# Queries of the first three batches loaded four tokens to a row, in a retention and bilinear feed-forward kernel

## The chip, the cores and the metric

One Trainium2 chip, one core. The time is device microseconds of one execution; the median of three runs of the kernel before is 325.34 us (325.18 to 326.11). The core has TensorE (matrix products, one instruction after another in the order of its queue), VectorE, ScalarE and GpSimd (elementwise work), and SyncE, which here only issues transfers. ScalarE and GpSimd issue transfers too. Each engine works through its own queue in order; an instruction that waits holds up everything behind it on that engine.

## What is computed

Eight batches, eight heads, 576 tokens, 64 features to a head, all inputs float32:

```
scores = q @ k^T / 8
gamma[h] = 1 - 2^(-5 - h)
D[h, s, t] = gamma[h]^(s - t)  for s >= t, else 0
x = (scores * D) @ v                      # per batch and head
x -> rows of 512 (all heads of a token), 4608 rows
out = ((x @ w_a) * (x @ w_b)) @ w_out     # 512 -> 1536 -> 512
```

## The kernel before, in words

The kernel works in bf16 with float32 sums. The decay is split: v is scaled by gamma^(-t) (table `vs`), the product's result by gamma^s / 8 (table `qs_o` for the first 256 tokens of a batch, `qs` later), and between them only a mask of zeros and ones is left. Attention runs in blocks of tokens; what lies in earlier blocks comes in through a running state (k^T v, 64 x 64 per head). The feed-forward part takes the resulting `xT` in blocks of 512, 256, 256 and then 512 tokens: products `pa` with `w_a` and `pb` with `w_b`, ScalarE copies `pa` out (L868), VectorE multiplies (L880), and `po` is the product with `w_out` (L896), copied out to `osb` and stored by SyncE. Attention of later batches is slipped into these products by a list of due times (`todo`), counted in TensorE cost.

**The opening.** The first 256 tokens of batches 0, 1 and 2 go another way than the rest, in steps: `STEPS` lists (batch, half of the heads); steps 0 and 2 are batch 0, steps 1 and 3 are batch 1, steps 4 and 5 are batch 2. Steps 0 to 3 are written out by hand, in the order in which the lines from L929 on stand; steps 4 and 5 are in `todo` (`early_casts`, `third_turn`, `third_states`, `third_outputs`). A step loads q, k and v of its four heads with two tokens to a row of SBUF: partition p holds tokens 2p and 2p + 1, 512 bytes together, so a transfer of 256 KB has 512 pieces of 512 bytes (L159). The steps' transfers stand in a row in SyncE's queue, except the first k, which ScalarE issues:

```
for i, which in ((0, Q), (0, K), (0, V), (2, Q), (2, K), (1, K),
                 (1, Q), (2, V), (3, K), (3, Q), (1, V), (3, V)):
```

Then, for each step: `cast_step` turns q and k into bf16, even tokens before odd ones (L316); `values_step` scales v (L324 on ScalarE, L326 elsewhere); `transpose_step` turns q and k, 128 x 128 at a time, on TensorE into PSUM (L334), and copies them out (L338); `score_step` makes 16 products of keys and queries (L352) and multiplies by the mask on VectorE (L360, `sT`); `state_step` makes k^T v (L379), and ScalarE copies the state that a later block needs (L391) and keeps sums (L395, L396); `output_step`, or its parts `open_step`, `step_states` (L449), `step_keys` (L465) and `close_step` (L481, L486), makes the outputs and writes them scaled into `xT`. Even tokens stand before odd ones everywhere, in the mask, in `qs_o`, in `xT` and so in the rows of `osb`; `store` undoes it with two transfers of 64 rows, every second row of the output (L791).

`last_states` makes the state products of steps 1 and 3 together and copies them out (L412 to L416). After the outputs of steps 1 and 3 the first feed-forward products begin: `ffn_begin` for the first 256 tokens (batch 0), `begin_with` for the next 256 (batch 1), both L811, with the first piece of `w_a`; the first `pb` (L875) follows.

`warm` puts products of ones into TensorE's queue (L923), whose results nobody reads. The weights are loaded in pieces through GpSimd's queue (`load_w`, `load_wo`), cast to bf16 on the way, in an order that stands between GpSimd's casts and value products.

PSUM: `ps_ffn` has four buffers of one bank for everything tagged `ab`; `ps_sc` and `ps_o` have one buffer of two banks each (the scores of a step, and the outputs of a step or the first two `pa`).

Of the kernel before, what the change touches and what calls it, by code (L numbers as in the profile page):

```python
# [10 lines left out]
FP32 = mybir.dt.float32  # L11
# [7 lines left out]
def kernel(  # L19
# [134 lines left out]
    def load_step(n, hh, which, on=nc.sync):  # L154

        if n not in paired:
            paired[n] = [stage.tile([128, 2 * DM], FP32, tag=name, name=name)
                         for name in ("qf", "kf", "vf")]
        on.dma_start(  # L159
            paired[n][which][:, hh * DM:(hh + 1) * DM]  # L160
            .rearrange("p (h e) -> p h e", h=4),
            (q, k, v)[which][n, 4 * hh:4 * hh + 4, 0:256, :]
            .rearrange("h (p two) d -> p h (two d)", two=2))
# [3 lines left out]
    for i, which in ((0, Q), (0, K), (0, V), (2, Q), (2, K), (1, K),  # L167
                     (1, Q), (2, V), (3, K), (3, Q), (1, V), (3, V)):
# [7 lines left out]
    idx_o = sum_pool.tile([128, 2, 2, 64], INT32, tag="sums", name="idx_o")  # L176
    nc.gpsimd.iota(idx_o, pattern=[[128, 2], [1, 2], [2, 64]], base=0,
                   channel_multiplier=0)
    identity = const.tile([128, 128], BF16)
    make_identity(nc, identity)  # L180
    mask_s = const.tile([128, 2, 2, 64], BF16)
    nc.gpsimd.memset(mask_s, 1.0)
    for a in (0, 1):
# [3 lines left out]
            pattern=[[-1, 2], [1, 2], [2, 64]], channel_multiplier=-2)  # L187
# [24 lines left out]
    for h in range(H):  # L212
# [6 lines left out]
    nc.vector.tensor_copy(qs_o[:, HP - 1],  # L219
                          idx_o.rearrange("p u k x -> p (u k x)"))  # L220
# [76 lines left out]

    def place_step(i):
# [3 lines left out]
        transposed[key] = half_of(qkt_pool, i, [2, DM], BF16, "qkT")  # L302

# [11 lines left out]
    def cast_step(i, w, on):  # L315
        COPY[on](by_parity(natural[STEPS[i]][0][:, w]), given(i, w))  # L316
# [12 lines left out]
    def transpose_step(i, *ways):  # L329
        qkb, qkT = natural[STEPS[i]][0], transposed[STEPS[i]]  # L330
        tp = ps_ffn.tile([128, len(ways), 4, 128], BF16, tag="ab", name="tp")
        for to, (w, on) in enumerate(ways):
            for c in range(4):
                nc.tensor.transpose(tp[:, to, c, :],  # L334
                                    qkb[:, w, c * 128:c * 128 + 128],
                                    identity)
        for to, (w, on) in enumerate(ways):
            COPY[on](qkT[:, w], tp[:, to].rearrange("p c x -> p (c x)"))  # L338

    def queries(key, r, j, a):  # L340
        return transposed[key][r, 0].rearrange(
            "p (k j s) -> p j k s", k=2, j=2)[:, j, :, half(a)]

    def score_step(i, place=None, tag="sc"):
# [3 lines left out]
        for j in (0, 1):  # L348
# [14 lines left out]
            mask_s.rearrange("p k q s -> p (k q s)").unsqueeze(1)  # L363
# [39 lines left out]
    def last_states():  # L403

        own, later_half = kvs = [
            ps_ffn.tile([128, 2, 2, 64], FP32, tag="ab", name=f"kv1{a}")
            for a in (0, 1)]
        fresh = set(QUADS)
        for i in (1, 3):
            state_products(i, [kv[:, i // 2] for kv in kvs], fresh)  # L410
# [372 lines left out]
    def store(u, cols, osb):  # L783
        n, u = place(u // 2), u % 2
        for kp, r0, m, b, s0 in rows_of(n):
# [3 lines left out]
            if n < FIRST:  # L789
                for par in (0, 1):  # L790
                    nc.sync.dma_start(rows[par::2], osb[half(par), cols])  # L791
            else:
                nc.sync.dma_start(rows, osb[r0:r0 + m, cols])
# [136 lines left out]
    make_qs(qs_o, 0, 0, 256)  # L930
    for i in range(4):
        place_step(i)
    cast_step(0, Q, "dve")
    cast_step(0, K, "dve")
    make_qs(qs_o, 1, 0, 256)
    transpose_step(0, (Q, "act"))
    transpose_step(0, (K, "dve"))
    values_step(0, 0, nc.scalar)
    values_step(0, 1, vector)
    make_qs(qs_o, 2, 0, 256)  # L940
    cast_step(2, Q, "pool")
# [3 lines left out]
    state_step(0)  # L945
    transpose_step(2, (Q, "dve"))
    cast_step(2, K, "pool")
    cast_step(1, K, "pool")
    warm(2, 512)
    transpose_step(2, (K, "dve"))  # L950
    warm(2, 512)
    load_w(*pieces[0], "a")
# [188 lines left out]
```

## Time and profile before

| | |
|---|---|
| time, median of 3 runs | 325.34 us |
| time of the profiled execution | 325.76 us |
| its span, first to last instruction | 324.0 us |
| TensorE busy | 318.6 us, 98% |
| VectorE, ScalarE, GpSimd busy | 165.5, 130.8, 118.8 us |
| hardware transfers (q, k, v, stores) | 45.37 MB, 68.2% of 16 engines' span |
| software transfers (weights) | 4.72 MB, 9.3% |
| first product of ones on TensorE | 1.52 us |
| first feed-forward product (L811) | 16.86 us |
| first `pb` (L875) | 18.60 us |

In a line of a timeline the first number is the start in us, the second the duration; then come engine, line, operation, what is written from what, shapes, and how many instructions are merged into the line. In square brackets stands how long the engine had been idle, and what ended that. A duration of TensorE merges overlapping instructions. In a DMA view the line with packets gives bytes and mean rate over the window asked for.

### The profile page before, as it was taken

The numbers are of one execution on the slowest core, as the hardware profiler recorded it, in microseconds if no ns is written. First come the engines' busy times: TensorE is split into PE (matmuls) and PEld (weight loads), VectorE is DVE, ScalarE is ACT, GpSimd is POOL, SyncE is SP. The second block draws the span as 40 slices with busy tenths as digits, with TensorE's granted clock in tenths as the row PEclk, the third lists the DMA queues.
The fourth block names the chain that finished last, engine by engine and source line by source line (L and its number), as shares of the span: only waits on it lengthen the run. The fifth ranks groups of instructions, "written<-read, shape, count | busy, mean of one in ns | idle before, by whom it ended". The sixth has DMA issues, their size and how long they took to land.

```text
span 324.0 us, 8659 instructions
## 1 busy us (share of the span) xinstructions
PE 318.6 (98%) x3607; PEld 164.4 (51%) x3607; DVE 165.5 (51%) x296; ACT 130.8 (40%) x289; POOL 118.8 (37%) x159
## 2 busy tenths in 40 slices
PE   8899999999999999999999999999999999999996
PEld 3554457777444554444454545454545444444444
DVE  4845345665546754835374627562566256514321
ACT  6745653435435523533253324442433343313321
POOL 3990076583745375457075205450520000000000
PEclk9999999999999999999999999999999999999999
DMA  8999999999999999999999168935750510031003
GB/s 215 253 202 207 261 229 195 197 181 197 182 223 243 218 192 240 229 223 230 182 211 195 47 156 194 214 78 144 169 113 15 141 42 2 2 97 32 1 23 109
DMA packets 146487, 50.90 MB, mean 157 GB/s; under 512 B 126736, under 2 KB 141968, under 8 KB 146448
## 3 DMA queue, kind: packets, MB, share of 16 engines
q1 hardware_dynamic: 140112, 45.37, 68.2%
q0 software_dynamic: 5808, 4.72, 9.3%
q8 instruction: 28, 0.46, 0.6%
q10 hardware_dynamic: 528, 0.26, 0.3%
q14 instruction: 11, 0.09, 0.1%
HBM read 37.75 MB, written 9.44 MB: 146 GB/s over the span
## 4 chain that ended last, share of the span: by engine, by line
PE 97%; ACT 1%; DVE 1%; issue 0%; DVEq 0%
PE pb L875 29%; PE pa L860 28%; PE po L896 28%; PE w L923 2%; PE po L822 2%; PE sc L635 2%; PE o L663 1%; PE o L676 1%; PE kv L573 1%; PE tp L334 1%; PE sc L352 1%; PE pa L811 1%; PE o L465 0%; ACT qkT L338 0%; ACT vb L324 0%
## 5 line engine op out<-in xcount | busy, mean ns | idle before, releaser
L880 DVE TENSOR_TENSOR hT<-ha,pb 128x512 bf16<-128x512 bf16 (+1 forms) x120 | 75.7, 632 | 93.7 <-PE pb L875 86.2
L875 PE MATMUL pb<-xT,wb_sb 128*128 128x512 bf16 (+1 forms) x480 | 111.6, 358 | 0.1
L868 ACT CAST ha<-pa 128x512 bf16<-128x512 f32 (+1 forms) x120 | 64.8, 543 | 113.6 <-PE pa L860 110.7
L860 PE MATMUL pa<-xT,wa_sb 128*128 128x512 bf16 (+1 forms) x472 | 109.8, 357 | 0.0
L896 PE MATMUL po<-wo_sb,hT 128*128 128x512 bf16 (+2 forms) x432 | 91.8, 367 | 0.0
L875 PEld LDWEIGHTS <-wb_sb 128*128 128x128 bf16 x480 | 46.9, 98 | 46.6 <-issue 0.3
L860 PEld LDWEIGHTS <-wa_sb 128*128 128x128 bf16 x472 | 45.4, 98 | 45.1 <-issue 0.4
L896 PEld LDWEIGHTS <-hT 128*128 128x128 bf16 x432 | 40.4, 98 | 44.4
L519 POOL CAST qkb<-qf 64x1024 bf16<-64x1024 f32 x15 | 15.4, 1030 | 68.2 <-DMA qf<-in_q_dram 57.9
L530 POOL TENSOR_TENSOR vb<-vf,vs 128x1024 bf16<-128x1024 f32 (+1 forms) x17 | 28.8, 1699 | 15.4 <-DMA vf<-in_v_dram 6.4
L907 DVE COPY osb<-po 128x512 f32<-128x512 f32 (+2 forms) x16 | 10.4, 649 | 39.1 <-PE po L896 39.1
L905 ACT COPY osb<-po 128x512 f32<-128x512 f32 (+1 forms) x20 | 11.4, 572 | 46.4 <-PE po L896 46.4
L519 POOL CAST qkb<-kf 64x1024 bf16<-64x1024 f32 (+1 forms) x17 | 15.9, 933 | 12.4 <-DMA kf<-in_k_dram 12.0
L598 DVE TENSOR_TENSOR sums<-kv,sums 128x256 f32<-128x256 f32 x44 | 18.6, 423 | 2.7 <-PE kv L573 0.8
L644 DVE TENSOR_TENSOR sT<-sc,mask 128x512 bf16<-128x512 f32 x30 | 19.5, 680 | 0.0
L523 POOL CAST qkb<-kf 64x512 bf16<-64x512 f32 (+1 forms) x34 | 18.6, 573 | 1.0
L523 POOL CAST qkb<-qf 64x512 bf16<-64x512 f32 x30 | 17.6, 614 | 0.6
L602 ACT CAST states<-sums 64x512 bf16<-64x512 f32 x26 | 16.0, 617 | 0.3
L689 DVE TENSOR_TENSOR xT<-o,qs 128x512 bf16<-128x512 f32 x24 | 15.4, 680 | 1.5 <-PE o L676 1.5
L923 PE MATMUL w<-ones 128*128 128x512 bf16 x19 | 7.4, 512 | 1.5 <-DVE idxp_f L204 1.5
L316 POOL CAST qkb<-kf 128x512 bf16<-128x512 f32 x4 | 2.4, 612 | 15.8 <-DMA kf<-in_k_dram 15.8
L360 DVE TENSOR_TENSOR sT<-sc,mask_s 128x1024 bf16<-128x1024 f32 x6 | 7.2, 1219 | 1.9 <-PE sc L352 1.8
(96 smaller groups left out, 173.4 us busy)
## 6 DMA issues: line engine op xcount, KB each, us to landing
qf<-in_q_dram SPq DMA_DIRECT2D x32, 256.0 KB, 4.8
vf<-in_v_dram SPq DMA_DIRECT2D x32, 256.0 KB, 5.1
kf<-in_k_dram SPq DMA_DIRECT2D x31, 256.0 KB, 4.8
out_dram<-osb SPq DMA_DIRECT2D x25, 256.0 KB, 2.5
out_dram<-osb SPq DMA_DIRECT2D x21, 128.0 KB, 2.7
wo_sb<-in_moe_w_out_dram POOLq DMA_DIRECT2D x3, 512.0 KB, 15.9
qf<-in_q_dram SPq DMA_DIRECT2D x8, 128.0 KB, 3.2
kf<-in_k_dram SPq DMA_DIRECT2D x8, 128.0 KB, 3.3
```

What stands on the lines that cost most here:

```text
L519: nc.gpsimd.tensor_copy(qkb[0:64, w, e], t[0:64, e])
L523: nc.gpsimd.tensor_copy(to[:, :, 1 - r], fro[:, :, r])
L530: nc.gpsimd.tensor_tensor(vb[:, e].rearrange("p (h d) -> p h d", d=D), t[:, e].rearrange("p (h d) -> p h d", d=D), decay[:, at], op=ALU.mult)
L598: nc.vector.tensor_tensor(sums[:, i], own, prev, op=ALU.add)
L602: nc.scalar.copy(to(half(1 - r)), fro(half(r)))
L644: nc.vector.tensor_tensor(sT[:, on].rearrange("p c k s -> p (c k) s"), sc[:, on].rearrange("p c k s -> p (c k) s"), mask3.unsqueeze(1).to_ ...
L689: nc.vector.tensor_tensor(x_of(t0, 128).rearrange("p c (a s) -> p c a s", a=2), o[:, :, :, kp].rearrange("p a c s -> p c a s"), qs[:, :, s ...
L860: nc.tensor.matmul(pa[:, 0:n], wa_sb[:, c, fs], xT[:, c], start=(c == 0), stop=(c == NC - 1))
L868: nc.scalar.copy(ha[:, 0:n], pa[:, 0:n])
L875: nc.tensor.matmul(pb[:, 0:n], wb_sb[:, c, fs], xT[:, c], start=(c == 0), stop=(c == NC - 1))
L880: nc.vector.tensor_tensor(hT[:, F, 0:n], has[F][:, 0:n], pb[:, 0:n], op=ALU.mult)
L896: nc.tensor.matmul(po[:, 0:width], hT[:, F, u * 128:(u + 1) * 128], wo_sb[:, F, cols], start=(F == 0), stop=(F == NF - 1))
```

## The change

For the first 256 tokens of batches 0, 1 and 2, q is loaded with four tokens to a row: 64 partitions hold one half of the heads (token 4p to 4p + 3, 1,024 bytes together), the other 64 partitions the other half, so that one batch fills one tile by two transfers. k and v are loaded as before. A cast of q now takes two of the four tokens of all eight heads (`cast_queries`, twice for a batch), and the eight transposes of a batch (`turn_queries`) give for each token of four and each pair of heads a 128 x 128 block whose copy out of PSUM is written with a step of four elements, which puts the queries into token order. With that the mask's columns, `qs_o`, `xT` and `osb` are in token order, and the rows of these batches are stored as all others are: one transfer of 128 rows in place of two of 64.

`turn_keys` does for k what `transpose_step` did. The order of the transfers, of the opening's lines and of the engines that do them is written anew: two warm products fewer; the first values on GpSimd; both q casts of batch 1 behind one another's data; `last_states` taken apart, with the output products of step 1 before the state products of step 3; and the first eight feed-forward products ahead of the state products of steps 1 and 3 (`step_states`) and their `close_step`.

```diff
+        src = (q, k, v)[which][n, 4 * hh:4 * hh + 4, 0:256, :]
+        if which == Q:
+            on.dma_start(
+                paired[n][Q][half(hh)].rearrange("p (h e) -> p h e", h=4),
+                src.rearrange("h (p four) d -> p h (four d)", four=4))
+            return
...
-    for i, which in ((0, Q), (0, K), (0, V), (2, Q), (2, K), (1, K),
-                     (1, Q), (2, V), (3, K), (3, Q), (1, V), (3, V)):
+    for i, which in ((0, Q), (0, K), (2, Q), (0, V), (2, K), (1, Q),
+                     (3, Q), (1, K), (2, V), (3, K), (1, V), (3, V)):
...
-            pattern=[[-1, 2], [1, 2], [2, 64]], channel_multiplier=-2)
+            pattern=[[-1, 2], [1, 128]], channel_multiplier=-2)
...
+        if i % 2 == 0:
+            heads_q[i // 2] = shared["qkb"][:, :, Q]
+            turned_q[i // 2] = shared["qkT"][:, :, Q]
...
+    def cast_queries(n, kk, on):
+        COPY[on](by_parity(heads_q[n][:, kk]),
+                 paired[n][Q].rearrange("p (h k d) -> p h k d", h=4, k=4)
+                 [:, :, 2 * kk:2 * kk + 2])
...
+    def turn_queries(n, on):
+        tp = ps_ffn.tile([128, 2, 4, 128], BF16, tag="ab", name="tpq")
+        for tok in range(4):
+            for j in (0, 1):
+                c0 = (tok % 2) * 256 + j * 128
+                nc.tensor.transpose(tp[:, j, tok, :],
+                                    heads_q[n][:, tok // 2, c0:c0 + 128],
                                     identity)
+        for j in (0, 1):
+            COPY[on[j]](turned_q[n][:, j].rearrange("p (x k) -> p k x", k=4),
+                        tp[:, j])
...
     def queries(key, r, j, a):
-        return transposed[key][r, 0].rearrange(
-            "p (k j s) -> p j k s", k=2, j=2)[:, j, :, half(a)]
+        n, hh = key
+        t0 = 256 * hh + 128 * a
+        return turned_q[n][r, j, t0:t0 + 128]
...
-            if n < FIRST:
-                for par in (0, 1):
-                    nc.sync.dma_start(rows[par::2], osb[half(par), cols])
-            else:
-                nc.sync.dma_start(rows, osb[r0:r0 + m, cols])
+            nc.sync.dma_start(rows, osb[r0:r0 + m, cols])
```

The opening's lines after the change, from the first load's cast on:

```
    warm(8, 512)
    for c in range(3):
        make_qs(qs_o, c, 0, 256)
    for i in range(4):
        place_step(i)
    cast_keys(0, "dve")
    cast_queries(0, 0, "dve")
    cast_queries(0, 1, "act")
    turn_keys(0, "dve")
    turn_queries(0, ("act", "dve"))
    values_step(0, 0, pool_)
    values_step(0, 1, pool_)
    make_qs(qs_o, 3, 0, 256)
    cast_keys(2, "pool")
    warm(2, 512)
    score_step(0)
    warm(1, 512)
    keeps = []
    state_step(0, keeps)
    turn_keys(2, "act")
    load_w(*pieces[0], "a")
    cast_queries(1, 0, "pool")
    cast_queries(1, 1, "act")
    warm(2, 512)
    score_step(2)
    keeps.pop()()
    cast_keys(1, "pool")
    open_step(0)
    step_states(0, True)
    step_keys(0, {0})
    warm(2, 512)
    turn_queries(1, ("act", "act"))
    turn_keys(1, "dve")
    close_step(0)
    values_step(2, 0, pool_)
    values_step(2, 1, pool_)
    load_w(*pieces[0], "b")
    warm(2, 512)
    score_step(1)
    cast_keys(3, "act")
    state_step(2, keeps)
    turn_keys(3, "act")
    open_step(2)
    step_states(2, True)
    step_keys(2, {0})
    values_step(1, 0, pool_)
    load_w(*pieces[1], "a")
    values_step(1, 1, nc.scalar)
    keeps.pop()()
    values_step(3, 0, vector)
    values_step(3, 1, pool_)
    load_w(*pieces[1], "b")
    score_step(3)
    close_step(2)
    kvs = [ps_ffn.tile([128, 2, 2, 64], FP32, tag="ab", name=f"kv1{a}")
           for a in (0, 1)]
    fresh = set(QUADS)
    for i, banks in ((1, ps_ffn), (3, ps_sc)):
        state_products(i, [kv[:, i // 2] for kv in kvs], fresh)
        open_step(i, banks)
        step_keys(i, {0, 1})
    last_copies(kvs)
    firsts = ps_o[0].tile([128, 2, 512], FP32, tag="o", name="pa2")
    for F in range(WCOLS[0]):
        ffn_begin(F, firsts[:, F])
    for i in (1, 3):
        step_states(i, False)
    for i in (1, 3):
        close_step(i)
    for c in (0, 1):
        for F in range(WCOLS[0]):
            begin_with(F, c, 1)
```

The third batch: its two q loads stand ahead of its k and v loads; `early_casts` and the entry at due time 112.1 cast the first and second pair of tokens on ScalarE; `third_turn` calls `turn_queries(2, ("act", "act"))` and then `turn_keys` of steps 4 and 5, each with a PSUM buffer of its own, in place of two `transpose_step`.

## The prediction

> **What bounds the kernel now.** I read four views in this order: the page (who is busy, what the chain is made of), TensorE's timeline over the first 26 us, the timelines of VectorE, ScalarE and GpSimd beside it, and last the DMA view in windows.
>
> The page, parts 1 and 4:
>
> ```profile
> PE 318.6 (98%) x3607; PEld 164.4 (51%) x3607; DVE 165.5 (51%) x296; ACT 130.8 (40%) x289; POOL 118.8 (37%) x159
> ...
> PE 97%; ACT 1%; DVE 1%; issue 0%; DVEq 0%
> ```
>
> TensorE is the bound. Once the feed-forward products run, nothing else ends the chain, so what can move is when they start, and whether something stops them later. The opening on TensorE (start, duration, line, tiles, count):
>
> ```profile
> 1.52 3.59 PE L923 MATMUL w<-ones 128*128 128x512 bf16 x8 [1.52 <-DVE idxp_f L204]
> 5.08 1.06 PE L334 MATMUL tp<-identity,qkb 128*128 128x128 bf16 x8
> ...
> 16.62 0.40 PE L449 MATMUL o<-qkT,state_after 128*128 128x128 bf16 x4
> 16.86 1.91 PE L811 MATMUL pa<-xT,wa_sb 128*128 128x256 bf16 x16
> 18.60 1.89 PE L875 MATMUL pb<-xT,wb_sb 128*128 128x512 bf16 x8
> ```
>
> I measure the opening by the start of the first `pb`, 18.60 us: from there TensorE runs without a gap. Note that the 16 products of L811 run unbroken from 16.86. What paces the steps before that, on VectorE, ScalarE and GpSimd:
>
> ```profile
> 4.59 0.43 DVE L316 CAST qkb<-qf 128x512 bf16<-128x512 f32 x1 [1.30 <-DMA qf<-in_q_dram]
> ...
> 7.68 1.22 DVE L360 TENSOR_TENSOR sT<-sc,mask_s 128x1024 bf16<-128x1024 f32 x1 [0.75 <-PE sc L352]
> ...
> 10.40 1.23 DVE L360 TENSOR_TENSOR sT<-sc,mask_s 128x1024 bf16<-128x1024 f32 x1 [0.53 <-PE sc L352]
> ...
> 14.76 1.23 DVE L360 TENSOR_TENSOR sT<-sc,mask_s 128x1024 bf16<-128x1024 f32 x1 [0.53 <-PE sc L352]
> 15.90 0.68 DVE L486 TENSOR_TENSOR xT<-o,qs_o 128x512 bf16<-128x512 f32 x1
> 16.50 0.87 DVE L481 TENSOR_TENSOR xT<-o,qs_o 128x256 bf16<-128x256 f32 x2
> ```
> ```profile
> 6.96 0.61 POOL L316 CAST qkb<-qf 128x512 bf16<-128x512 f32 x1 [3.90 <-DMA qf<-in_q_dram]
> 7.78 0.61 POOL L316 CAST qkb<-kf 128x512 bf16<-128x512 f32 x1 [0.21 <-DMA kf<-in_k_dram]
> ```
> ```profile
> 15.80 0.75 ACT L412 CAST state_after<-kv 64x256 bf16<-64x256 f32 x2 [0.34 <-PE kv L379]
> ```
>
> The first Q is in at 4.59, the fourth transfer (Q of the other four heads) at 6.96, then one about every 0.9 us. The DMA view from 5 to 12 us, and two windows late in the run, around one whole 256 KB store (286.45 to 287.19) and around two stores of 64 rows (289.3 to 290.6):
>
> ```profile
> DMA packets 4091, 2.03 MB, mean 290 GB/s; under 512 B 125, under 2 KB 4091, under 8 KB 4091
> ```
> ```profile
> DMA packets 136, 0.26 MB, mean 349 GB/s; under 512 B 10, under 2 KB 10, under 8 KB 136
> ```
> ```profile
> DMA packets 148, 0.26 MB, mean 199 GB/s; under 512 B 22, under 2 KB 22, under 8 KB 148
> ```
>
> At 290 GB/s 256 KB take 0.90 us. The same bytes in the same 2 KB packets took 0.74 us from 128 rows and 1.3 us from twice 64.
>
> **The loads.** Q now lands on 64 partitions per transfer, with 1 KB packets. No row shows that. Bounds: as cheap as the whole store, 0.74 us; as dear as the two half stores, 1.3 us. I take 1.2, near the half stores, because loads into 64 partitions are here too: the last pairs' 128 KB K and V loads ran at 190 GB/s from 193 to 199 us (in part for lack of issues), where whole ones reach 290. Q of both head halves is needed before any of it is cast. The second Q is third in line now, ahead of the first V, and shares its start with K on ScalarE's queue; the third transfer of before arrived at 6.0 (0.9 ahead of the fourth), and I take 6.0 (4.8 if Q goes at 350 to 400 GB/s, 6.3 if at 200). The two Q of the second batch cost 0.3 us more each, so the last V comes at about 14.7 instead of 14.0 (bounds 13.4 and 15.7). The first weights were issued at 9.24, yet the window from 5 to 12 us holds no packet of the software queue: they flow only when the loads drain. So they shift with the last V, from 16.2 to about 16.9, and are hidden as long as the first product starts after that. That `wa` is now issued one cast earlier gains nothing for this reason; `wb` is issued about 1.5 us later, behind later values, and hidden behind `wa`'s stream.
>
> The Trainium skill, SBUF — State Buffer, section Door 1: The DMA port swizzle, says that 64 adjacent partitions reach 8 of the 16 DMA ports, and gives 196 GB/s for them against 328 for 128 at 1 MiB. The 199 against 349 GB/s above agree; by its rate Q would take 1.3 us, by the whole store's row 0.74.
>
> **The chain of the opening, after.** Laid out in queue order with the rows' durations, 0.05 us from one engine to the next. The same reckoning for the kernel before gives 18.5 where the trace has 18.60. Cast of half the queries on ScalarE (0.61, beside K's and the other half on VectorE, 0.43 each) 6.05 to 6.65. Eight transposes: 1.06 us at the early pace (0.107 us apart; later ones are 0.055 apart) to 7.7. Copies out, one half on ScalarE 0.59, one on VectorE: 0.42 as contiguous copy, now with a step of four elements, bounded by 0.42 and the 0.65 of an f32 PSUM copy of that size (L907); I take 0.65 since a strided write has no reason to be faster. To 8.4. Scores 0.64 to 9.1, so the first mask product starts at 9.2 instead of 7.68: 1.5 us late. What was two transfers, casts and copies side by side (Q from 4.59) now begins at 6.0 and is one thing behind the other.
>
> Then the engines' own order paces it. Behind the scores stand one warm product and the key-value products to 9.5; ScalarE's state copies (0.5) and then K's copy of the other step (0.59) to 10.65; scores, second mask product at 11.2 (10.40 before). ScalarE's cast of the second batch's queries stands behind that copy, 10.6 to 11.2, although its data is there by about 10.2; TensorE comes to those transposes at 11.8, two warm products in front; both copies are on ScalarE (0.50 and 0.59) to 13.6; third mask product 14.1 (12.67 before). ScalarE again: K's cast to 14.1, state copies to 14.8, K's copy to 15.4; fourth mask product 15.9 to 17.1 (from 14.76 before). The value product that now stands before it on VectorE waits for the last V, 14.7 plus 0.41: over at 15.3, hidden. It is uncovered once V lands after 15.4. The close of batch 0 (0.68) ends at 17.7 and lets the first product go at 17.8, 0.94 later than 16.86.
>
> **The end of the opening.** The first eight L811 products (0.86) now stand before the four state products, not behind. The ScalarE state copy they were to cover is over by 18.2, and the products themselves end at 18.7. In turn they no longer cover the closes: the state products end at 18.95, the half close that needs them (0.43) at 19.4, the next close (0.68) at 20.0, and only then come the last four products (0.43). `pb` starts at 20.5. From first product to `pb` it is 2.7 us where it was 1.74, so about 0.95 is lost here wherever the first stands.
>
> Sum: 20.5 less 18.5 in the same reckoning is +2.0. If the transposes already run at the later pace, it is +1.6. I take +1.8. All later TensorE work moves by as much, and the weights, then 0.7 late, are ahead of it.
>
> **Hidden parts.** GpSimd's two first value products (0.6 each) end at about 8.1, before the key-value products at 9.2; the third exponential now before the first ScalarE cast ends at 5.0, ahead of the data. Two fewer warm products: nothing, they fill waits. Third batch: the same 16 transposes (at 43.64), copies 1.07 on ScalarE and 0.91 on VectorE as now, scores at 45.5; one more PSUM buffer of four is held, 0 to +0.4 us; I take 0, as the `osb` copy that must free it ends at 43.67. Its loads, Q first and 0.3 longer each, put the last V 0.7 later; TensorE 1.8 later covers that. Stores: twelve of 64 rows become six whole ones, some 0.6 us less each for SyncE; no TensorE wait on a DMA is in the list of waits, so nothing.
>
> **The rivals.** *The loads win* (other side): 1 KB packets on the hardware queue run like the whole store, 0.74 instead of 0.90; four Q save 0.65 us, weights and last V come 0.65 earlier, and the end of the opening follows the data: 324.7. For it speaks that the early steps wait for DMA; against it the 199 GB/s row and the queue order: `pb` beats 18.60 only if the first product starts by 15.9, that is the fourth mask product by 14.0, two us before my layout. *A wash*: second Q at 4.8 and TensorE at its later pace put the first mask product at 7.7; that is 1.5 earlier than laid, so `pb` comes at 19.0, +0.5: 325.9. For it: whole stores do reach 349 GB/s; against it: no load here went over 345, and that with two queues at once. *The data becomes the wall*: at 200 GB/s the last V lands at 15.7, the value product holds the fourth mask product back to 16.15 (+0.25), and the weights come at 17.8, no later than the first product; TensorE stays at the early pace until about 11 (+0.4: five more groups at double duration, in part covered), and the third batch pays its 0.4. With 1.8 that is +2.9: 328.2.
>
> The early pace: eight warm products took 3.59 us, 12 later ones of that size take 2.59 in the chain's rows. The Trainium skill, TensorE: Matmul & The Clock Gate, section What's actually happening, ties the change to a busy window of about 3.4 us. By that rule the 1 us in which TensorE now waits for the second Q may push the change back by a window; that is the last rival's term.
>
> **How the numbers follow.** The profiled run of before took 325.76 us for a span of 324.0; the median is 325.34, 0.42 less. On the median: 325.34 + 1.8 = 327.1. Chances: this forecast 0.60 (its own range 326.5 to 327.8: the pace, 0.4 either way, and 0.3 of the second Q's landing), the wall 0.20, the wash 0.13, the loads win 0.07. Leaving out the win and the far end of the wall, the range is 325.9 to 328.3. About 0.3% (0.98 us) is what a measurement of this kernel can tell from no change: faster 0.07, same 0.13, slower 0.80.
>
> **What would show it.** First mask product near 9.2, fourth near 15.9; L811 split in 8, 4 and 4 with gaps; `pb` near 20.5; a window with only Q loads near 200 GB/s. Wrong, if Q's transfer takes 0.75 us, if the second Q is cast before 5.2, or if a gap opens around 44 to 48 us.

## The result, and the profile after

The changed kernel takes 334.69 us (median of 6 runs, 334.09 to 336.41), the kernel before on the same chip 325.33 us. The ratio is 1.0293, with an interval of 1.0264 to 1.0322: 9.4 us slower, where 1.8 us were forecast. The direction was right, the size was off by a factor of five. The profiled run took 334.09 us for a span of 332.4 us, 8.4 us more span than before.

The page of the changed kernel, parts 1, 2 and 4 (busy times, the granted TensorE clock in 40 slices, the chain):

```profile
PE 320.3 (96%) x3605; PEld 165.5 (50%) x3605; DVE 166.6 (50%) x294; ACT 133.8 (40%) x287; POOL 119.4 (36%) x160
...
PEclk9599999999999999999999999999999999999999
...
PE 93%; ACT 2%; DVE 2%; DMA 2%; issue 0%; SPq 0%; DVEq 0%
```

TensorE is still the bound, but its share of the chain fell from 97% to 93%: ScalarE, VectorE and transfers hold 6% where they held 2%. The second slice of the clock, 8.3 to 16.6 us, shows a 5. The opening on TensorE:

```profile
4.91 0.41 PE L346 MATMUL tp<-identity,qkb 128*128 128x128 bf16 x4
7.25 0.62 PE L355 MATMUL tpq<-identity,qkb 128*128 128x128 bf16 x8 [1.93 <-DVE qkb L327]
...
9.26 0.43 PE L375 MATMUL sc<-qkT 64*64 64x128 bf16 x8 [0.95 <-ACT qkT L359]
10.58 0.43 PE L375 MATMUL sc<-qkT 64*64 64x128 bf16 x8 [0.90 <-DVE qkT L359]
...
22.55 1.03 PE L825 MATMUL pa<-xT,wa_sb 128*128 128x256 bf16 x8 [0.18 <-DVE xT L504]
23.42 0.39 PE L467 MATMUL o<-qkT,state_after 128*128 128x128 bf16 x4
24.21 1.20 PE L825 MATMUL pa<-xT,wa_sb 128*128 128x256 bf16 x8 [0.40 <-DVE xT L499]
25.24 1.89 PE L889 MATMUL pb<-xT,wb_sb 128*128 128x512 bf16 x8
```

The first `pb` comes at 25.24 instead of 18.60: 6.64 us of the 8.4 are lost before it. The scores, one group of products before, now stand in two halves, each behind a wait of 0.9 us, once for ScalarE's copy of the turned queries and once for VectorE's. The rows of VectorE and ScalarE say why:

```profile
9.24 1.29 DVE L359 COPY qkT<-tpq 128x512 bf16<-128x512 bf16 x1 [1.71 <-ACT qkT L359]
11.13 1.22 DVE L383 TENSOR_TENSOR sT<-sc,mask_s 128x1024 bf16<-128x1024 f32 x1 [0.60 <-PE sc L375]
13.92 1.23 DVE L383 TENSOR_TENSOR sT<-sc,mask_s 128x1024 bf16<-128x1024 f32 x1 [1.57 <-PE sc L375]
...
18.86 1.23 DVE L383 TENSOR_TENSOR sT<-sc,mask_s 128x1024 bf16<-128x1024 f32 x1 [1.60 <-PE sc L375]
...
20.67 1.23 DVE L383 TENSOR_TENSOR sT<-sc,mask_s 128x1024 bf16<-128x1024 f32 x1 [0.26 <-PE sc L375]
```
```profile
7.91 1.30 ACT L359 COPY qkT<-tpq 128x512 bf16<-128x512 bf16 x1 [0.54 <-PE tpq L355]
...
16.02 2.44 ACT L359 COPY qkT<-tpq 128x512 bf16<-128x512 bf16 x2 [2.07 <-PE tpq L355]
...
50.92 2.44 ACT L359 COPY qkT<-tpq 128x512 bf16<-128x512 bf16 x2 [1.07 <-PE tpq L355]
```

A copy of 128 x 512 takes 1.29 us on VectorE and 1.30 on ScalarE. The contiguous copy of the same size (L348, same kernel) takes 0.42 and 0.59. VectorE's copy does not run beside ScalarE's: it starts at 9.24, when ScalarE's (7.91 to 9.21) is over, although the transposes behind both are done by 7.87. In the second batch ScalarE makes both copies, 2.44 us where two contiguous ones take 1.07 (third batch of the kernel before), and in the third batch again, where TensorE waits for it in the midst of the feed-forward part:

```profile
53.42 0.31 PE L375 MATMUL sc<-qkT 64*64 64x128 bf16 x8 [0.83 <-ACT qkT L359]
```

Matched product by product from the last one back, TensorE is 6.64 us behind the kernel before at the first `pb`, 7.8 behind the third batch's scores and 8.0 at the last product; the last 0.4 us of span lie behind that product (experiments 8 and 9). What is left of the 9.4 us are the medians: the profiled run is the shortest of the six, 0.6 us under their median, and the profiled run of the kernel before was 0.4 us above its own.

### The profile page after: what moved, and what is told of

It reads as the page before. It is cut to its first block, busy times and chain, and to the rows that moved or that the text cites. A ratio compares the mean times of both kernels' runs of the same rounds, so it can differ in the third digit from the quotient of the medians.

```text
span 332.4 us, 8641 instructions
## 1 busy us (share of the span) xinstructions
PE 320.3 (96%) x3605; PEld 165.5 (50%) x3605; DVE 166.6 (50%) x294; ACT 133.8 (40%) x287; POOL 119.4 (36%) x160
## 4 chain that ended last, share of the span: by engine, by line
PE 93%; ACT 2%; DVE 2%; DMA 2%; issue 0%; SPq 0%; DVEq 0%
PE pb L889 28%; PE pa L874 28%; PE po L910 27%; ACT qkT L359 2%; PE po L836 2%; DMA qf<-in_q_dram 2%; PE sc L653 1%; PE o L694 1%; PE o L681 1%; PE kv L591 1%; PE sc L375 1%; PE pa L825 1%; PE w L937 1%; PE tpq L355 0%; PE o L483 0%; DVE qkT L359 0%
## 5 line engine op out<-in xcount | busy, mean ns | idle before, releaser
L537 POOL CAST qkb<-kf 64x1024 bf16<-64x1024 f32 (+1 forms) x17 | 15.9, 933 | 13.0 <-DMA kf<-in_k_dram 12.4
```

Source lines behind the costliest of these rows:

```text
L537: nc.gpsimd.tensor_copy(qkb[0:64, w, e], t[0:64, e])
```

## The experiments

Theory A, formed from these rows: the copies, dear because they write with a step, and one behind the other because both read one PSUM buffer, cost most. Rival B: the loads of q on 64 partitions. Rival C: the order of the opening, its end above all. Beside them, D: the granted clock, which fell to half from 8.37 to 15.19 us.

**1. The step on the reading side.** The same copy with the step in the read of PSUM; the write is a row.

```diff
-            COPY[on[j]](turned_q[n][:, j].rearrange("p (x k) -> p k x", k=4),
-                        tp[:, j])
+            COPY[on[j]](turned_q[n][:, j].rearrange("p (x k) -> p x k", k=4),
+                        tp[:, j].rearrange("p k x -> p x k"))
```

> The copies of the turned queries read PSUM with a step (token block by token block) and write 512 elements in a row, instead of reading in a row and writing with a step of four; the result is the same. Theory A (the write's step makes the copy dear: 1.30 us, where the flat copy of that size has 0.59 on ScalarE and 0.42 on VectorE, and two stand one behind the other on the chain in the opening for each batch, and once more in the third batch): copies at about 0.6, first pb at 22.0 to 22.8 instead of 25.2, no gap of 0.83 before the scores of the third batch, 330.5 to 331.5 us in all. Theory B (any step is dear, read or written): copies stay at 1.3 and the time at 334 to 335. Theory C (the loads into 64 partitions and the clock carry the loss): copies may get shorter, the time falls by less than 1.5.

Measured: 329.88 us, ratio 1.0130 (1.0068 to 1.0192), 4.8 us below the changed kernel (4.7 by the spans of the profiled runs). Its timelines of ScalarE, VectorE and TensorE:

```profile
8.42 0.59 ACT L359 COPY qkT<-tpq 128x512 bf16<-128x512 bf16 x1 [0.95 <-PE tpq L355]
```
```profile
9.04 0.69 DVE L359 COPY qkT<-tpq 128x512 bf16<-128x512 bf16 x1 [1.41 <-ACT qkT L359]
10.33 1.23 DVE L383 TENSOR_TENSOR sT<-sc,mask_s 128x1024 bf16<-128x1024 f32 x1 [0.60 <-PE sc L375]
```
```profile
22.11 1.89 PE L889 MATMUL pb<-xT,wb_sb 128*128 128x512 bf16 x8
```

ScalarE pays nothing for the step in the read (0.59), VectorE 0.27 (0.69 against 0.42). `pb` comes 3.1 us earlier and the third batch no longer holds TensorE: the lag behind the kernel before is 3.5 us ahead of it and behind it. So the written step is about half of the whole loss.

**2. No step at all.** Both sides contiguous; the queries stay out of token order, so the scores are those of other tokens. It bounds what any cheaper reordering could still bring.

```diff
-            COPY[on[j]](turned_q[n][:, j].rearrange("p (x k) -> p k x", k=4),
-                        tp[:, j])
+            COPY[on[j]](turned_q[n][:, j],
+                        tp[:, j].rearrange("p k x -> p (k x)"))
```

> The same copies flat on both sides, so the queries are left in the order of the transposes (the reordering is left out, tokens end up in the wrong place). Theory A: copies 0.59 on ScalarE and 0.42 on VectorE, the same time as with the step on the read side within 0.5 us. Theory B: this one alone falls, to 330.5 to 331.5. Theory C: less than 1.5 us gained.

Measured: 329.87 us, ratio 1.0117 (1.0070 to 1.0164), the same as experiment 1. VectorE's row:

```profile
8.77 0.42 DVE L359 COPY qkT<-tpq 128x512 bf16<-128x512 bf16 x1 [1.41 <-ACT qkT L359]
```

The 0.27 us that the read step costs VectorE do not show in the time. With a contiguous copy 4.2 us of loss are still there (the kernel before took 325.68 beside it), so the price of the copies is not all.

**3. The old loads alone.** q loaded as before, 512 bytes to a piece on 128 partitions; the rest is the changed kernel, copies included. The number of partitions and the size of a piece change together here. The rows land in the wrong places, so it computes with misplaced queries.

```diff
-                paired[n][Q][half(hh)].rearrange("p (h e) -> p h e", h=4),
-                src.rearrange("h (p four) d -> p h (four d)", four=4))
+                paired[n][Q][:, hh * DM:(hh + 1) * DM]
+                .rearrange("p (h e) -> p h e", h=4),
+                src.rearrange("h (p two) d -> p h (two d)", two=2))
```

> q of the first three batches loaded as before the change, two tokens to a row on 128 partitions with 512-byte pieces, all else as after (the casts then take the wrong tokens; the placing is left out). Theory A: the second Q is in at 6.0 instead of 6.7, the last V at 14.0 instead of 16.5; the opening ends 0.6 to 1.0 earlier, since the copies and ScalarE's order pace it: 333.5 to 334.2. Theory C (loads carry the loss): pb by 22.5, 331.5 to 332.5.

Measured: 333.58 us, ratio 1.0235 (1.0186 to 1.0285), 1.1 us below the changed kernel by the medians; the two sets of runs overlap (333.2 to 335.0 beside 334.1 to 336.4). The DMA view of the changed kernel from 4 to 6.6 us, when it moves the two Q, and of this one from 4 to 5.8:

```profile
DMA packets 833, 0.52 MB, mean 200 GB/s; under 512 B 30, under 2 KB 833, under 8 KB 833
```
```profile
DMA packets 1098, 0.54 MB, mean 303 GB/s; under 512 B 34, under 2 KB 1098, under 8 KB 1098
```

The second Q lands at 5.82 instead of 6.67, the last V at 13.98 instead of 16.55. Little of that reaches the time, with the dear copies behind it. The profiled run, the longest of the four, does not show the gain at all: its clock fell to half twice (8.88 to 15.71 and 19.12 to 25.95 us), and its `pb` starts at 26.46, later than in the changed kernel.

**4. The end of the opening as before.** The state products and the closes of steps 1 and 3 again ahead of the sixteen first feed-forward products.

```diff
+    for i in (1, 3):
+        step_states(i, False)
+    for i in (1, 3):
+        close_step(i)
     firsts = ps_o[0].tile([128, 2, 512], FP32, tag="o", name="pa2")
     for F in range(WCOLS[0]):
         ffn_begin(F, firsts[:, F])
-    for i in (1, 3):
-        step_states(i, False)
-    for i in (1, 3):
-        close_step(i)
```

> The four state products and the closes of batch 1 back ahead of the first eight feed-forward products, as before the change; all else as after. My reckoning: the products of L825 run unbroken again, first pb 0.7 to 1.0 earlier (24.2 to 24.5), 333.7 to 334.0 in all. Rival: the order is neutral there, because the state copy it was to cover then stands open: no more than 0.3 gained.

Measured: 334.55 us, ratio 1.0264 (1.0202 to 1.0327): 0.1 below the changed kernel, within the scatter of the two. TensorE:

```profile
22.97 0.40 PE L467 MATMUL o<-qkT,state_after 128*128 128x128 bf16 x4 [0.54 <-ACT state_after L430]
23.20 1.91 PE L825 MATMUL pa<-xT,wa_sb 128*128 128x256 bf16 x16
24.95 1.89 PE L889 MATMUL pb<-xT,wb_sb 128*128 128x512 bf16 x8
```

The sixteen products run unbroken, as before, yet `pb` comes only 0.29 earlier. The state products wait 0.54 us for ScalarE's state copies, which the eight products in the changed order had covered.

**5. Cheap copies and old loads.** Experiments 1 and 3 together (misplaced queries).

> The step on the read side (as in e1) and the 512-byte loads of q on 128 partitions together (the casts then take the wrong tokens; the placing is left out). With the dear copies gone the loads should show: second Q at 5.8 instead of 6.75, last V at 14.0 instead of 16.5. If the second Q paces the opening: 0.8 to 1.2 less than e1 (328.7 to 329.1). If the order of the engines' queues paces it: less than 0.4 below e1. What is then left above the kernel before (325.5) is the order.

Measured: 327.63 us, ratio 1.0066 (1.0049 to 1.0083), 2.25 us below experiment 1 by the medians, 1.8 by the spans of the profiled runs: once the copies are cheap, the loads show. `pb` at 20.35, 1.76 earlier than in experiment 1:

```profile
17.66 1.03 PE L826 MATMUL pa<-xT,wa_sb 128*128 128x256 bf16 x8 [0.18 <-DVE xT L505]
18.53 0.39 PE L468 MATMUL o<-qkT,state_after 128*128 128x128 bf16 x4
19.32 1.20 PE L826 MATMUL pa<-xT,wa_sb 128*128 128x256 bf16 x8 [0.40 <-DVE xT L500]
20.35 1.89 PE L890 MATMUL pb<-xT,wb_sb 128*128 128x512 bf16 x8
```

**6. A PSUM buffer for each half of the turned queries**, so that the two copies can run side by side (on top of experiment 1).

```diff
-        tp = ps_ffn.tile([128, 2, 4, 128], BF16, tag="ab", name="tpq")
+        tp = [ps_ffn.tile([128, 4, 128], BF16, tag="ab", name=f"tpq{j}")
+              for j in (0, 1)]
...
-                nc.tensor.transpose(tp[:, j, tok, :],
+                nc.tensor.transpose(tp[j][:, tok, :],
...
-                        tp[:, j].rearrange("p k x -> p x k"))
+                        tp[j].rearrange("p k x -> p x k"))
```

> e1 with a PSUM buffer of its own for each of the two halves of the turned queries; the result is the same. In after and e1 VectorE's copy starts only when ScalarE's, from the same buffer, has ended. If the common buffer is the reason, VectorE's copy now starts at 8.5 beside ScalarE's instead of 9.04, the second half of the scores follows the first at once, and the time is 0.3 to 0.6 below e1 (329.3 to 329.6). Rival: VectorE waits for something else, the copy starts at 9.04 as before, the time is that of e1 or, for the buffer more, 0.2 above.

Measured: 331.75 us, ratio 1.0172 (1.0139 to 1.0205): not faster than experiment 1. By the medians it is 1.9 us slower, but the two sets of runs overlap (330.3 to 332.7 beside 329.2 to 331.6). VectorE first, then TensorE:

```profile
7.79 0.69 DVE L360 COPY qkT<-tpq 128x512 bf16<-128x512 bf16 x1 [0.38 <-PE tpq L356]
9.13 1.23 DVE L384 TENSOR_TENSOR sT<-sc,mask_s 128x1024 bf16<-128x1024 f32 x1 [0.65 <-PE sc L376]
...
17.87 0.42 DVE L339 TENSOR_TENSOR vb<-vf,vs 128x256 bf16<-128x256 f32 x1 [1.98 <-DMA vf<-in_v_dram]
18.21 1.22 DVE L384 TENSOR_TENSOR sT<-sc,mask_s 128x1024 bf16<-128x1024 f32 x1
```
```profile
20.08 1.87 PE L826 MATMUL pa<-xT,wa_sb 128*128 128x256 bf16 x8
```

The mechanism is as supposed: VectorE starts at 7.79, beside ScalarE (7.73), waits for TensorE instead of ScalarE, and the first mask product comes at 9.13 instead of 10.33. What held it back is a wait that the program carries: with one tile VectorE's copy waits for a semaphore that ScalarE's copy raises. Then the opening, now 1.1 us ahead, runs into the last V: VectorE waits 1.98 us for it until 17.87 and holds the fourth mask product back to 18.21 (17.55 in experiment 1). That is my third rival's wall, by its mechanism. And the clock stood at half from 18.11 to 24.94 us, where the eight products took 1.87 us instead of 1.03. In this profiled run, the longest of the four, the fourth mask product is 0.66 us behind experiment 1 and `pb`, at 24.33, 2.22: the 1.56 between them fall in the stretch at half clock. The third batch takes another 1.0, where TensorE waits ahead of transposes of keys (0.52 us, at 51.02). Why the last V landed later than in the changed kernel (17.84 against 16.55) the run does not settle; the first packet of the weights came earlier, at 12.54 instead of 13.34.

**7. TensorE kept busy** in the changed kernel: four warm products ahead of the first `turn_queries`, and four for two ahead of the first scores.

> After, with four more warm products ahead of the first queries' transposes and two more ahead of the first scores, where TensorE stands idle for 1.9 and 0.9 us; nothing else. If it is the idle time that lets the clock fall (half from 8.4 to 15.2 us in the profile of after), the granted clock stays at full speed, the groups between run at their later pace, and the time is 0.7 to 1.5 below after (333.2 to 334.0). Rival: the clock's fall costs nothing, since copies pace these steps: within 0.4 of after.

Measured: 333.66 us, ratio 1.0246 (1.0231 to 1.0261), 1.0 below the changed kernel (0.6 by the spans of the profiled runs). The clock was full from 6.24 to 19.90 us, and the mask products came earlier, the first at 10.87 (11.13 in the changed kernel), the fourth at 19.22 (20.67). Then the clock fell to half until 23.31, and `pb` came only 0.36 earlier. So in this run the fall was moved, not taken away.

**8. Token order in the kernel before.** Its loads, its order and its stages, but the copy of the turned queries puts them into token order by a step in the read, and the rows are stored whole. The mask, the tables, `queries` and the store are changed to match, as in the change itself; the cut shows the copy alone.

```diff
-        for to, (w, on) in enumerate(ways):
-            COPY[on](qkT[:, w], tp[:, to].rearrange("p c x -> p (c x)"))
+        for to, (w, on) in enumerate(ways):
+            if w == K:
+                COPY[on](qkT[:, w], tp[:, to].rearrange("p c x -> p (c x)"))
+            else:
+                COPY[on](qkT[:, w].rearrange("p (j x k) -> p j x k", j=2, k=2),
+                         tp[:, to].rearrange("p (k j) x -> p j x k", k=2))
```

> The kernel before with only the token order of the change: q, k and v loaded as before, all orders as before, but the copy of the turned queries puts them into token order (PSUM read with a step, written in a row), mask and tables to match, and the rows of the first three batches stored whole, one transfer instead of two. The result is the same. My reckoning: ScalarE's copies keep 0.59, VectorE's go from 0.42 to about 0.7 (twice in the opening, 0.1 to 0.3 on the chain), the stores move nothing on TensorE: 325.2 to 326.0, the same as before. Rival: whole stores free the transfers for the loads behind them: 0.5 or more below before.

Measured: 325.79 us, ratio 1.0007 (0.9997 to 1.0016): no change. Token order and whole stores together move the time by less than can be told. One thing did not fit: the last product of TensorE came 0.30 us earlier than in the kernel before, and the span was 0.1 us longer. Of the 0.30, 0.26 are there at `pb` (18.34); full clock came at 6.27 in this profile and at 7.42 in that of the kernel before, which may be the reason, though no run shows it.

**9. Twelve stores instead of six** in that kernel: each of the six whole stores as two of 64 rows.

```diff
-            nc.sync.dma_start(rows, osb[r0:r0 + m, cols])
+            if n < FIRST:
+                for h in (0, 1):
+                    nc.sync.dma_start(rows[half(h)], osb[half(h), cols])
+            else:
+                nc.sync.dma_start(rows, osb[r0:r0 + m, cols])
```

> The kernel before with token order and read-step copies, but each of the six whole stores of the first three batches sent as two stores of 64 rows, twelve in all as before. Nothing on TensorE, VectorE or ScalarE differs from e8_token_order. In every kernel with whole stores the span ran 1.34 us on from the last landing, in the kernel before 0.97: SyncE checks the semaphores of the transfers one pair after the other at the end, 0.062 us each, and stops at the one that lands last, which is the second of nine where there are six fewer transfers and the eighth before. Theory A, the number of stores decides on which semaphore the last store lands: 0.97 us from the last landing to the end, six checks less, span 323.7, median 0.3 to 0.4 us below e8_token_order (325.79), that is 325.4, no different from the kernel before. Rival B, the tail comes from something else in the whole-row order: 1.34 us as in e8, median 325.8 or more, since two half stores cost SyncE 0.6 us more each.

Measured: 325.43 us (325.38 before on the same chip; experiment 8 had 325.79 beside 325.54), ratio 1.0008 (0.9991 to 1.0025). The times do not tell the two stores apart; the trace does: the span is 323.6 us instead of 324.1. SyncE's last instructions, from the trace's records (start in us, semaphores checked), the last landing marked:

```
experiment 8, six whole stores               experiment 9, twelve half stores
321.615  118, 117                            321.464  118, 117
         last landing 322.758 (100)          321.534  100, 116
322.775  100, 116                            ...
322.837  102, 115                            321.948  107, 111
322.901  104, 114                                     last landing 322.628 (108)
...                                          322.644  108, 101
323.204  109, 110                            322.706  109, 110
323.269  end of the checks                   322.771  end of the checks
```

At the end SyncE checks the semaphores of all transfers, pair by pair, 0.062 us each, in a fixed order, and stops at the one that has not yet come. Eight of them serve the loads and stores in turn. With six stores fewer the last store lands on semaphore 100, second in the list, and eight checks are made after it; with the old number it lands on 108, and two are. From the last landing to the end of the span it is 1.33 to 1.35 us in every kernel here with six stores, and 0.97 in both with twelve. This is the last 0.37 us of the changed kernel's loss.

**10. The end of the opening again, with cheap copies and old loads** (the edit of experiment 4 on experiment 5; misplaced queries).

> The changed kernel with the read-step copy, the old loads of q (rows to the wrong partitions, so the output is not the reference's) and the state products with the two closes put back ahead of the sixteen first feed-forward products. Beside e5_step_and_512, where the first product to pb took 2.69 us (17.66 to 20.35). Theory A, my prediction's 0.95 us for the eight products put ahead holds where ScalarE is not late: the sixteen products run unbroken, start at about 17.6 to 17.9, pb at 19.4 to 19.6, median 0.8 to 0.95 below e5's 327.63, at 326.7 to 326.9. Rival B, as in e4_states_first: the state products stand and wait for ScalarE's state copies, the start slips by 0.65, pb at 20.0, median 0.3 below, 327.3.

Measured: 327.42 us, ratio 1.0061 (1.0048 to 1.0075), 0.21 below experiment 5, and hardly a difference by the ratios. TensorE:

```profile
18.12 0.40 PE L468 MATMUL o<-qkT,state_after 128*128 128x128 bf16 x4 [0.57 <-ACT state_after L431]
18.35 1.91 PE L826 MATMUL pa<-xT,wa_sb 128*128 128x256 bf16 x16
20.10 1.89 PE L890 MATMUL pb<-xT,wb_sb 128*128 128x512 bf16 x8
```

Rival B holds: the sixteen products start at 18.35, not 17.66, because the state products wait 0.57 us for ScalarE. `pb` comes 0.25 us earlier than in experiment 5: that is what the order of the end costs.

**11. Cheap copies and TensorE kept busy** (the edit of experiment 7 on experiment 1).

> e1_read_step with four warm products put ahead of the first turning of queries, and four instead of two ahead of the first scores. In the changed kernel such products gave 1.0 us, where the granted clock had fallen to half between 8.4 and 15.2 us. In e1_read_step TensorE idles 1.8 us before that turning and the clock came up only at 10.8 us. Theory A, the clock is a term of its own also with cheap copies: full clock from about 7.5 to 8.5 us, the steps from 7.4 to 10.8 us shorter, pb at 21.6 to 21.8 (22.11 without), median 0.3 to 0.5 below 329.88. Rival B, with cheap copies the waits of the opening hide the slower products: pb within 0.15 of 22.11, median within 0.2.

Measured: 329.83 us, ratio 1.0151 (1.0121 to 1.0181): no different from experiment 1. Full clock came at 5.70 us instead of 10.72, and `pb` at 21.40 instead of 22.11, the way that A said. How much of that the four products did is open: when full clock first comes differs from run to run, and in the changed kernel, without them, it came at 4.95. The gain went again in the third batch:

```profile
47.76 0.40 PE L346 MATMUL tp<-identity,qkb 128*128 128x128 bf16 x4 [0.49 <-DVE qkT L348]
```

Two things end just ahead of these transposes: VectorE's copy of the step before, which the row names (47.31 to 47.74), and GpSimd's cast of their own k (47.09 to 47.70), late because GpSimd had waited for the third batch's first k until 45.05. In experiment 1 the same transposes did not wait for that copy of VectorE (they ran at 47.59, it at 48.02), so k is the likelier; no run took it away. Behind the gap the lag to the kernel before is 3.45 us, as in experiment 1 (3.5): the opening gave 0.7 us, and the third batch took it back. The 0.7 also bear on experiment 5: its profile has full clock from 4.60, that of experiment 1 from 10.72, so part of the 1.76 between their `pb` may be the clock. Beside experiment 11 it is 1.05.

## Why the prediction was wrong, step by step

The median's 9.4 us, by differences of medians, in the order in which the runs take the change apart: the written step 4.8 (changed kernel to experiment 1), the loads of q on 64 partitions 2.25 (1 to 5), the order at the end 0.2 (5 to 10), the number of stores 0.37 (by the trace, 8 and 9), and 1.6 left between experiment 10, less that 0.37, and experiment 9. By the spans of the profiled runs the first three parts are 4.7, 1.8 and 0.1. The runs were made on several chips, with the kernel before between 325.3 and 325.7 us beside them, and the ratio of experiment 1 is known to 0.6% (2 us) either way, so the parts are rough. They are not independent either: while the copies were dear, the loads alone were worth 1.1 by the medians, within the scatter.

| step | predicted | measured |
|---|---|---|
| second Q lands | 6.0 | 6.67 |
| copies of turned queries, first batch | 0.59 beside 0.65 | 1.30, then 1.29 |
| first mask product | 9.2 | 11.13 |
| second, third, fourth | 11.2, 14.1, 15.9 | 13.92, 18.86, 20.67 |
| first feed-forward product | 17.8 | 22.55 |
| from it to `pb` | 2.7 | 2.69 |
| `pb` | 20.5 | 25.24 |
| third batch | 0 (to 0.4) | 1.15 |
| stores | 0 | 0, and 0.37 at the end for their number |

**The copy's price was the step that failed.** "I take 0.65 since a strided write has no reason to be faster": the reason named is about a lower end, and 0.65 was used as if it were the upper one. No row of the trace before wrote 2-byte elements with a gap, so the upper bound was not a bound. Measured: 1.29 us for 512 columns, 2.52 ns a column, on VectorE; 2.54 on ScalarE; 0.82 and 1.15 contiguous. The Trainium skill, Vector Engine (DVE) Microarchitecture Reference, section 5.2 Measured stream behaviour on trn2, has rows for a destination that moves away at every element, measured there with 4-byte words in SBUF: 1.71 ns a column for hops of 4 KiB, 2.50 to 2.51 for steps of 24 words. The trace agrees with the upper one, for 2-byte elements out of PSUM and a step of 8 bytes, and ScalarE shows the same price, of which those rows do not speak. An estimate from that page would have been 0.9 to 1.3 us; this was the page to weigh against the row.

**The two copies side by side failed too.** I laid VectorE's copy beside ScalarE's. Both read one PSUM tile, and the second waited for the first in every run with one tile (experiments 1 and 2 with cheap copies as well), and no longer with two (experiment 6). The trace of the kernel before had this in its third batch, the one place where it copies a turned tile with both engines; its opening, where I read the copies, has a tile for each:

```profile
44.91 0.91 DVE L338 COPY qkT<-tp 128x512 bf16<-128x512 bf16 x2 [1.24 <-ACT qkT L338]
```

The two errors add up: 2.6 us from the first copy's start to the second's end, where 0.65 were reckoned.

**"Both copies are on ScalarE (0.50 and 0.59)"** was 2.44 us, 1.35 more. The lag behind the times of the prediction grew by 2.0, from 2.7 us at the second mask product to 4.8 at the third; the rest of that growth came ahead of these transposes, in products at half clock. The same two copies stand in the third batch, where "I take 0" became 1.15; experiment 1 takes that loss away and leaves everything else there, so it was the copies and not the PSUM buffer that I weighed.

**The second Q: transfer right, landing mis-sized.** Two Q alone ran at 200 GB/s, 1.3 us for 256 KB, near the 1.2 taken. But the landing at 6.0 was read off the third transfer of before, ahead of which two ran at full rate. The first Q was slow as well (it landed at 5.00, 4.57 before), so the landing moves twice by about 0.4: 6.7. That is 0.7 of the first mask product's 1.9 us.

**The clock.** I had it only as the last rival's 0.4. TensorE reached full clock at 4.95 us (7.42 in the kernel before), and so the first transposes of queries took 0.62 instead of 1.06 us: the later pace, for which the prediction had 0.4 less and took half of it. That was luck: with the same products on TensorE up to that point, full clock first came at 10.72 in experiment 1 and at 13.14 in experiment 2. Then the waits for the second Q and the copies came, and it stood at half from 8.37 to 15.19. This table by stretches of the changed kernel (length; busy time and count of TensorE, weight load, VectorE, ScalarE, GpSimd; granted clock; DMA share and GB/s) shows it:

```profile
4.95:8.37 3.42, 1.43 (x15) 0.86 (x14) 0.76 (x2) 1.08 (x2) 0.78 (x2) 1.00 1.08 239
8.37:11.78 3.41, 1.63 (x33) 0.81 (x32) 1.94 (x2) 1.16 (x2) 2.10 (x4) 0.50 1.17 227
11.78:15.19 3.41, 3.41 (x54) 1.71 (x43) 1.80 (x2) 1.96 (x6) 3.08 (x6) 0.50 1.28 258
```

The stretch with 1.43 us of work is followed by half clock, the one with 3.41 by full; but the next one, 15.19 to 18.60, with 1.85 us of work, kept full clock. The steps are 3.41 us long, as the Trainium skill has it for its activity window (TensorE: Matmul & The Clock Gate, What's actually happening). The Trainium skill's rule against a fall on the same page, no idle gap over about 3.4 us (section HAM oscillation — how this bites in real kernels), is too mild for this case: the longest gap ahead of the fall here was 1.93 us, and 0.42 in the stretch ahead of the second fall of experiment 6 (14.70 to 18.11). What a fall costs is known only roughly: keeping TensorE busy was worth 0.6 to 1.0 us in experiment 7, and at most 0.7 at `pb`, nothing at the end, in experiment 11. The single runs of experiment 1 differ by more: 329.2 and 329.4 us with a mean clock of 1.000, 330.4 and 331.6 with 0.995.

**The end of the opening: the duration right, the loss wrong.** "About 0.95 is lost here wherever the first stands." From first product to `pb` it took 2.69 us, as laid out. But in the old order the start would have slipped, since ScalarE's state copies end late: 0.54 and 0.57 us of wait in experiments 4 and 10. The net loss is 0.25 to 0.3. My own layout had it: the state copy over at 18.2, 0.4 behind the first product at 17.8. I did not charge the old order with that wait.

**Hidden parts.** The exponentials, GpSimd's first values and the weights stayed hidden, as said. But "they flow only when the loads drain" failed: from 13 to 16.6 us the software queue moved 0.36 MB beside the hardware queue's 0.47, and the last V came at 16.55 instead of 14.7. In all thirteen traces the first packet of the weights came 3.1 to 4.1 us after its issue, with the loads nearly done (the kernel before, 0.04 MB left) or not (the changed kernel, 0.37 MB left). In the changed kernel nothing waited for the last V, because all else was later still; in experiment 6 it became the wall.

**The rivals.** The loads did not win (200 GB/s, not 349), and a wash was far off (its sum, 325.34 + 0.5, is 325.8, not 325.9). The wall had the transfer's price and the third batch's loss in it, but for another reason, and its 328.2 was the dearest that I thought possible. What was missing among the rivals was one on the copies: everything that the change does to the chain goes through them.

Still open: the 1.6 us between experiments 10 and 9. In experiment 10 the first mask product starts at 8.86, in experiment 9 at 7.20, so the whole of it is there by then, with loads of the same shape in both; the need for both Q ahead of the first transposes and the two copies in a row lie between. They were not tried apart.

## What to carry to other kernels

When a reordering has to be paid somewhere, write contiguously and put the step into the read: here 0.59 to 0.69 us against 1.30 for 128 x 512 bf16 out of PSUM. Before two engines' copies are laid side by side, look whether they read the same tile; and where the trace has no row for an access pattern, leave the upper bound open or find a price elsewhere, above all if the operation stands in the chain two or three times. A step removed from one place of a tuned opening shows only as far as the next wall, here the last V, the clock or, as it seems, the third batch's k.

## What the runs showed of the hardware that was not expected

- A written step of four bf16 elements costs 2.5 ns a column on VectorE and ScalarE alike (1.29 and 1.30 us for 512); the same step in the read costs ScalarE nothing (0.59) and VectorE 0.27 us.
- The granted clock falls to half for 3.41 or 6.83 us behind stretches of that length with 1.34 to 1.87 us of TensorE work (the changed kernel and experiments 3, 4 and 6), but also behind ones with 2.52 and 2.67 (experiments 7 and 6), while 1.85 in the changed kernel (15.19 to 18.60) and 2.08 and 2.55 in experiment 5 kept it. No threshold can be read from this. The stretches also lie differently in each run: full clock first comes between 4.46 us (experiment 6) and 13.14 (experiment 2), with TensorE busy from 1.52 in all.
- The number of transfers in a program moves its end: 0.062 us for each pair of semaphores that SyncE still checks after the last landing, 0.37 us between six stores and twelve.
